# A fused attention and MLP block on one core: activation tables fetched ahead, first transposes in two banks, a Silu gate for the last tokens, and a new order

## The chip, the core and the metric

The kernel runs on one core of a Trainium2 chip. The core has a matrix engine (PE, with PEld for its weight loads), a vector engine (DVE), an engine for activation functions (ACT), GpSimd (POOL), and SyncE (SP), which here only issues transfers. The metric is the time of one launch in device microseconds; less is better.

## The reference

Input x is 2048 tokens of 448 values. With xn = layernorm(x), two branches are computed and joined:

```
A: q, k, v = xn @ wqkv             16 heads of 28
   token s attends to s, s-2, s-4, ... s-14 (those >= 0), softmax
   s = attention output @ wo
B: h = gelu_tanh(xn @ w1 + b1)     1792 hidden values
   g = silu(h @ w2 + b2)
out = x + s * g                    bf16 in and out
```

## The kernel before

Tokens are taken even ones first, then odd ones, so that a token attends to itself and its seven neighbours to the left. They form 16 tiles of 128 and four chunks of four tiles.

**The work.** For each tile: load, statistics on DVE (`bn_stats`), 1/sqrt(var) on ACT (chunk 0) or POOL (later chunks), xn on DVE, and xn transposed: by PE for the four tiles of chunk 0, by a transposing transfer of SP's queue for the others. Then the projections q, k and v (lines 532 and 556). q and k are copied out of PSUM to `qk_tok` and transposed by SP's queue to `qkT`; v is copied to `v_tok` and moved by POOL's transfers to where attention wants it.

ff1 makes h for a chunk of 512 tokens in 14 hidden tiles (line 591), gelu on ACT (595). ff2 (line 627) makes 448 outputs for one tile of tokens out of 14 hidden tiles; then `y` = that plus b2 on DVE (649), `t` = tanh(y/2) on ACT (655), `g` = (t+1)*y on DVE (659), which is twice silu(y). The last tile is cut into two halves of 224 columns.

Attention works on nine blocks of 228 tokens (block 4: 224). A visit S of PE makes the scores of a block in four banks (677); ACT takes exp (687) into `E`, POOL or DVE multiplies by the mask (693). A visit P makes the outputs in two banks, one for each window of 114 tokens (709). For each window DVE does four steps: transpose, reciprocal, transpose, multiply into `oT` (719, 723, 728, 733). A final (796) multiplies `oT` of a tile by wo; DVE makes `sg` = 0.5 * that * g (801) and `o` = x + sg (807), SP writes it out (811).

**PE's tile shapes.** The first batch of projections, transposes, ff2, finals and warm-ups use the whole array (128 rows). The other projections and ff1 run two at a time on its halves (64 rows): a `pair` has four steps, then a no-op on POOL or SP that passes a semaphore on (the hop), then three steps. Scores use 32 rows and 64 columns, attention outputs 64 rows and 32 columns.

**PSUM.** There are eight banks. A matmul task takes banks, and the evacuation gives them back.

**The order.** The kernel records tasks with costs, priorities (`PRIO`, `LATER`) and dependencies; a planner (`_Plan.run`) gives every task an engine and a place with a model of the times, and the instructions are written out in that order. On an engine nothing overtakes. So a change of a cost in the model moves instructions, though the cost itself issues none. The stages are: ff1 of chunks 0 and 1, attention of chunks 0 to 2, ff1 of chunk 2, attention of chunk 3, ff1 of chunk 3; ff2 and finals fill in.

**ACT's tables.** sqrt, gelu and exp each need a function table; tanh is in those of exp and gelu. A load is written right before the first activation that needs another table. `state["gate"]` and `exps` make the first exp of a stage wait for all gelus before it, and ff1 for all exps before it.

**Warm-up.** At the start PE runs matmuls on zeros, up to a planned time of 8 us (line 327).

Of the kernel before, what the change touches and what calls it, by code (L numbers as in the profile page):

```python
# [13 lines left out]
HOP = 0.10  # L14
# [6 lines left out]
MASK_ON = (("DVE", "POOL"), (0.4, 1.2))  # L21
# [23 lines left out]
class _Plan:  # L45
# [29 lines left out]
    def _at(self, t, e, free):  # L75
        at = free.get(e, 0.0)
        for p, n in t.take.items():
            if len(p.free) < n or p.fifo and p.fifo[0] is not t:
                return None
            at = max(at, sorted(p.free)[n - 1][0] + HOP)  # L80
        if t.table and self.table not in t.table:
            at += TABLE
        for d in t.deps:
            at = max(at, d.end - d.tail if d.on == e else d.end + HOP)
        if e == "PE" and t.mode != self.mode:
            at = max(at, free.get(e, 0.0) + SWITCH)
        return at

    def run(self):
# [9 lines left out]
        while ready:  # L99
            cand = []  # L100
            for t in ready:
                ways = []
                for e, c in zip(t.eng, t.cost):
                    at = self._at(t, e, free)
                    if at is not None:
                        ways.append((at + (c if len(t.eng) > 1 else 0.0), at, e, c))
                if ways:
                    _, at, e, c = min(ways)
                    cand.append((at, t, e, c))
            if not cand:  # L110
                raise RuntimeError("the plan is stuck: " + str([(t.seq, t.eng, t.fn.__qualname__) for t in ready[:20]]))
            first = min(cand, key=lambda k: k[0])
            near = [k for k in cand if k[2] == first[2] and k[0] <= first[0] + SLACK]
            tiled = first[2] == "PE" and self.mode < 64
            at, t, e, c = min(near, key=lambda k: (-k[1].prio - (TILED if tiled and k[1].mode < 64 else SAME if k[2] == "PE" and k[1].mode == self.mode else 0),
                                                   k[0], k[1].seq))
            if t.limit is not None and at > t.limit:
                t.fn, c = None, 0.0
            t.on, t.start = e, at
            if e == "PE" and t.fn is not None:  # L120
                self.mode = t.out or t.mode
            if t.table and self.table not in t.table:
                self.table = t.table[0]
            free[e] = at + c
            t.end = at + c + t.tail
            for p, n in t.take.items():
                got = sorted(p.free)[:n]
                for g in got:
                    p.free.remove(g)
                t.slots[p] = [g[1] for g in got]  # L130
                if p.fifo is not None:
                    p.fifo.pop(0)
            for p, owner, i in t.give:
                p.free.append((t.end, owner.slots[p][i]))
            ready.remove(t)
            order.append(t)
            for u in t.users:
                u.ndep -= 1
                if not u.ndep:
                    ready.append(u)  # L140
# [24 lines left out]
def kernel(  # L165
# [13 lines left out]
    P = 128  # L179
# [66 lines left out]
    def ring(name, n, shape, dt=BF16, fifo=False):  # L246
# [24 lines left out]
        "project": (49.5, 205, 104, 52.5,),  # L271
        "project2": (147, 150, 101, 61,),
        "values": (89.5, 62.5, 21, 58,),
        "attn": (185, 179.5, 78, 174.5, 106.5, 106, 138.5, 136.5, 32.5,),
        "ff1": (185, 180, 84.5, 176.5, 66.5, 64.5, 156.5, 189.5, 203, 146, 76, 114.5, 77.5, 179.5,
            75.5, 118.5, 180.5, 14.5, 163, 68, 151, 115.5, 194.5, 167.5, 180, 188.5, 86, 93,),
        "gelu": (62.5, 22.5, 95, 92.5,),
        "ff2": (144, 162.5, 103.5, 142.5, 44.5, 112.5, 67, 5, 89, 106.5, 101.5, 75, 74, 55, 11.5,
            6.5,),
        "final": (140, 19.5, 70.5, 47, 112, 34.5, 23.5, 142.5, 73, 53, 198.5, 188.5, 81.5, 126.5,  # L280
            180, 71,),
        "norm": (37.5, 132, 179.5, 129.5, 74.5, 99, 161, 69, 63, 62, 43.5, 73, -5.5, 90, 133.5,
            150,),
        "loads": (166.5, 166, 188, 139.5, 54.5,),
        "stats": (47.5, -60, 180.5, 23, 127, 56, 188.5, 77, 197.5, -13.5, 185, 205.5, 138, 14, 52.5,
            138.5,),
        "turn_x": (108.5, -1, 28, 116, 210, 116.5, 131.5, 160, 41.5, 79.5, 70, 119, -4.5, 74.5,
            132.5, 111,),
        "turn_qk": (68.5, 112, 174.5, 90, 80, 6, 149.5, 60.5, 4, 140.5, 199.5, 96.5, 103, 166.5,
            140, 156,),  # L290
        "move_v": (81.5, 95, 23, 95, 18.5, 26.5, 8, 128, 29.5,),
        "copies": (50, 119.5, 58.5, 76, 32.5, 135.5, 43, 1, 87, 79.5, 129, 77, 32, 41.5, 135,),
    }
    LATER = {"swap": 135, "qk": 165, "v": 29.5, "gelu": 30.5, "exp": 55.5, "mask": -60, "pv": 45, "recip": -16.5, "os": 54.5, "y": 153.5, "tanh": 182.5, "g": 58, "sg": 183, "o": 120.5}
# [28 lines left out]
    t_on = plan.add("DMA", 0.8, lambda _: None, (), 100)  # L323
# [6 lines left out]
    t_eps = plan.add("DVE", 0.07, memset("vector", eps_t[:], EPS), [t_on], prio=99)  # L330
    t_eps = plan.add("DVE", 0.07, memset("vector", half_t[:], -0.5), [t_eps], prio=99)
# [7 lines left out]
    t_qz = [plan.add("DVE", 0.08, memset("vector", q[:, :, :, DH:], 0.0), [t_on], prio=95) for q in qk_tok]  # L339
    t_vw = [plan.add("DVE", 0.08, memset("vector", v[:, :, DH:], 1.0), [t_on], prio=96) for v in v_tok[:9]]  # L340
    t_row0 = plan.add("POOL", 0.1, memset("gpsimd", row0[:], 0.0), [t_on], prio=93)
    t_row0 = plan.add("POOL", 0.1, memset("gpsimd", row0[:1, :], 1.0), [t_row0], prio=93)
    t_wo = [plan.add("POOL", 1.0, memset("gpsimd", wo[:], 0.0), [t_on], prio=93)]

    def dma(eng, dst, src, kb, prio, deps=(), issue=0.5, rate=350.0):
        def fn(_):
            {"SP": nc.sync, "ACT": nc.scalar, "POOL": nc.gpsimd}[eng].dma_start(dst, src)
        a = plan.add(eng, issue, fn, [t_on] + list(deps), prio)
        return plan.add("DMA", kb / rate, lambda _: None, [a], prio, tail=1.7)
# [16 lines left out]
    def load_x(t0, n, prio, eng="SP", deps=()):  # L366
        d = dma(eng, x_sb[:, t0:t0 + n, :],
                rows(x_half, t0 * P, n * P).rearrange("(t p) d -> p t d", p=P), 112 * n, prio, deps,
                rate=270.0 if t0 < TPC else 350.0)
# [7 lines left out]
    load_x(0, 1, 300, "SP")  # L377
    load_x(1, 1, 300, "ACT")
    t_w = []

    def load_w(kt, prio):
        t_w.append([dma("SP", w_in[:, kt, :], A_wqkv[kt * P:(kt + 1) * P, :], 336, prio, rate=270.0)])
# [6 lines left out]
    t_w.append([dma("SP", w_in3[:64], tails[:, 0:3:2, :], 112, PRIO["loads"][3], rate=270.0),  # L389
                dma("SP", w_in3[64:], tails[:, 1:3, :], 112, PRIO["loads"][3], rate=270.0)])  # L390
# [7 lines left out]


# [11 lines left out]
    t_rs = {}  # L411

    def rstds(t0, n):
        if t0 < TPC:
# [6 lines left out]
            b = plan.add("DVE", 0.16, f2, [a], prio=290)  # L421
        else:
# [13 lines left out]
    def norm(t, prio):  # L436
# [11 lines left out]
        halves = []  # L448
        for i in range(2):
            def f3(k, i=i):  # L450
                xn, tp = buf(p_xn, a), half_bank(buf(p_b, (halves or [k])[0]))
                for kt in (2 * i, 2 * i + 1):
                    nc.tensor.transpose(tp[:, kt, :], xn[:, kt * P:(kt + 1) * P], ident[:])
            halves.append(plan.add("PE", 0.13 if t else 0.22, f3, [twice if i else a, t_ident] + halves, prio, take=() if i else (p_b,),
                                   give=((p_xn, a, 0),) if i else (), tail=0.15))
        b = halves[0]

        n = 2 if t < 2 else 4
        for k0 in range(0, KT, n):
            def f4(k, k0=k0):  # L460
                copy(k.on, xnT[:, k0:k0 + n, t * P:(t + 1) * P], half_bank(buf(p_b, b))[:, k0:k0 + n, :])
            t_xT[t] = plan.add(("DVE", "ACT"), (dve(n * P, 2), act(n * P)), f4, [halves[(k0 + n - 1) // 2]] + ([t_xT01[t]] if k0 else []), prio,
                               give=((p_b, b, 0),) if k0 + n == KT else ())
            t_xT01.setdefault(t, t_xT[t])

# [135 lines left out]

    t_g = {}
# [13 lines left out]
    def ff2_part(t, cs, n, end, prio):  # L616
# [36 lines left out]

        def f3(k):
            nc.scalar.activation(buf(p_t, k)[:, :n], buf(pool, y)[:, :n], ACT.Tanh, scale=0.5)  # L655
        th = plan.add("ACT", act(n), f3, after, prio + LATER["tanh"], take=(p_t,), table=("exp", "gelu"))
# [86 lines left out]
    def attn(b, what):  # L743

        deps, take, give, fns, cost = [], [], (), [], -SWITCH
        for n, (w, blk) in enumerate(what):
            if not n or what[n - 1][0] != w:
                cost += SWITCH
            cost += 0.215
            if not n:  # L750
                cost += 0.03
# [40 lines left out]
    def final_part(t, cs, n, g, prio):  # L792
# [7 lines left out]
        def f2(k):  # L800
            nc.vector.scalar_tensor_tensor(out=buf(p_sg, k)[:, :n], in0=buf(p_b, a)[:, :n], scalar=0.5,  # L801
# [10 lines left out]
        q = plan.add("SP", 0.55, f4, [o], 50)  # L812
# [24 lines left out]
    for m, w1_, n, first in ((m_gen, m1[0], NW, None), (m_first, m1[1], NW, 0), (m_mid, m1[2], NW - 1, 1)):  # L837
# [10 lines left out]
        t_m = plan.add("POOL", 1.2 if first is None else 1.6, fn, [t_ident], prio=75)  # L848
# [34 lines left out]
    b1_at = plan.add("PE", 0.06, f_b1, [t_b1r, t_ident], 60, take=(p_b,), tail=0.15)  # L883
# [24 lines left out]
    for i, (c, what) in enumerate(STAGES):  # L908
        if what == "A":
# [3 lines left out]
            if i + 1 == len(STAGES) or STAGES[i + 1][1] != "A":  # L913
                state["gate"], state["early"] = gels, gels[:-1]
# [3 lines left out]
        else:  # L918
            if was == "A":
                gels = []  # L920
            hs = [ff1(c, mt, PRIO["gelu"][c], exps) for mt in range(NMT)]
# [3 lines left out]
            if c == 0:  # L925
                project(2)
                project(3)
            for t in range(c * TPC, (c + 1) * TPC):
# [38 lines left out]
```

## Time and profile before

| | us |
|---|---|
| three runs | 158.65, 158.05, 158.40; median 158.4 |
| span of the profiled execution, first to last instruction | 156.2 |
| the profiled execution's own time | not shown apart from the runs; median less span is 2.2 |
| PE busy (share of the span) | 150.1 (96%) |
| DVE busy | 113.2 (72%) |
| ACT busy | 83.3 (53%) |
| POOL busy | 74.7 (48%) |
| mean granted clock of PE | 1.000 |

A row of the timeline gives start, length, engine, line, operation, tiles, shape and count; in brackets stands idle time of the engine before it and what ended it. Neighbouring rows of PE overlap, since matmuls are pipelined; the time from start to start is what a row costs. The chain of waits goes back from the last instruction to whatever released each step.

### The profile page before, as it was taken

The numbers are of one execution on the slowest core, as the hardware profiler recorded it, in microseconds if no ns is written. First come the engines' busy times: TensorE is split into PE (matmuls) and PEld (weight loads), VectorE is DVE, ScalarE is ACT, GpSimd is POOL, SyncE is SP. The second block draws the span as 40 slices with busy tenths as digits, with TensorE's granted clock in tenths as the row PEclk, the third lists the DMA queues.
The fourth block names the chain that finished last, engine by engine and source line by source line (L and its number), as shares of the span: only waits on it lengthen the run. The fifth ranks groups of instructions, "written<-read, shape, count | busy, mean of one in ns | idle before, by whom it ended". The sixth has DMA issues, their size and how long they took to land.

```text
span 156.2 us, 5305 instructions
## 1 busy us (share of the span) xinstructions
PE 150.1 (96%) x2204; PEld 77.8 (50%) x2204; DVE 113.2 (72%) x259; ACT 83.3 (53%) x149; POOL 74.7 (48%) x123
## 2 busy tenths in 40 slices
PE   6999999999999999999999999999999999999980
PEld 2544454444455555455554644455556444545570
DVE  4789551486266758997799895109899996998992
ACT  3245867378889416444634149782496587051220
POOL 7854856000459408839261098389599780000000
PEclk9999999999999999999999999999999999999999
DMA  4999969999749443099039822123300100200211
GB/s 156 329 317 315 167 124 187 237 269 307 141 95 166 64 82 90 10 192 138 4 83 85 131 70 73 38 76 83 105 0 4 34 31 29 63 4 0 68 36 43
DMA packets 33575, 17.36 MB, mean 111 GB/s; under 512 B 25331, under 2 KB 32387, under 8 KB 33552
## 3 DMA queue, kind: packets, MB, share of 16 engines
q1 hardware_dynamic: 31472, 14.03, 41.3%
q0 software_dynamic: 1936, 2.88, 8.5%
q8 instruction: 17, 0.28, 0.8%
q10 hardware_dynamic: 144, 0.11, 0.2%
q14 instruction: 6, 0.05, 0.1%
HBM read 7.06 MB, written 1.84 MB: 57 GB/s over the span
## 4 chain that ended last, share of the span: by engine, by line
PE 80%; DVE 8%; DMA 3%; POOL 2%; issue 2%; ACT 1%; SPq 1%; DVEq 0%; ACTq 0%; POOLq 0%
PE bank L627 23%; PE bank L591 22%; PE bank L532 11%; PE bank L796 7%; PE bank L556 6%; PE bank L677 4%; PE bank L709 4%; PE bank L327 3%; DMA xnT<-xn 3%; POOL v L354 2%; DVE sg L801 2%; DVE o L807 1%; DVE w_in L659 1%; ACT E L687 1%; DVE xn L438 1%
## 5 line engine op out<-in xcount | busy, mean ns | idle before, releaser
L627 PE MATMUL bank<-w,h 128*128 128x448 bf16 (+1 forms) x238 | 45.2, 342 | 0.0
L591 PE MATMUL bank<-xnT,w 64*128 64x512 bf16 x392 | 44.7, 376 | 0.0
L595 ACT ACTIVATE h<-bank,b 128x512 bf16<-128x512 f32 x56 | 34.0, 689 | 12.9 <-PE bank L591 12.8
L354 POOL DMA_DIRECT2D v<-v_tok x52 | 27.6, 538 | 19.8 <-PE bank L709 9.0
L693 POOL TENSOR_TENSOR E<-E,m_gen 128x456 bf16<-128x456 bf16 x24 | 26.7, 1139 | 11.7 <-ACT E L687 9.5
L627 PEld LDWEIGHTS <-h 128*128 128x128 bf16 x238 | 22.3, 98 | 18.1 <-issue 0.4
L591 PEld LDWEIGHTS <-w 64*128 64x128 bf16 x392 | 19.1, 94 | 22.7 <-issue 1.1
L532 PE MATMUL bank<-w_in,xnT 64*128 64x448 bf16 (+1 forms) x212 | 24.3, 350 | 0.1
L687 ACT ACTIVATE E<-bank 128x456 bf16<-128x456 f32 (+1 forms) x36 | 17.0, 555 | 9.1 <-PE bank L677 9.1
L655 ACT ACTIVATE t<-y 128x448 f32<-128x448 f32 x15 | 8.7, 578 | 17.4 <-DVE y L649 17.4
L719 DVE STREAM_TRANSPOSE dt<-bank 128x480 f32<-128x480 f32 (+1 forms) x18 | 12.1, 671 | 5.6 <-PE bank L709 5.6
L532 PEld LDWEIGHTS <-xnT 64*128 64x128 bf16 (+1 forms) x212 | 10.6, 94 | 10.9 <-issue 1.1
L314 DVE CAST qk_tok<-bank 128x448 bf16<-128x448 f32 x16 | 9.4, 613 | 6.8 <-PE bank L532 6.8
L796 PE MATMUL bank<-wo,oT 128*128 128x448 bf16 (+1 forms) x68 | 14.1, 342 | 0.0
L312 ACT CAST qk_tok<-bank 128x448 bf16<-128x448 f32 x16 | 8.3, 533 | 10.6 <-PE bank L532 10.0
L556 PE MATMUL bank<-w_in,xnT 64*128 64x448 bf16 (+1 forms) x106 | 13.4, 349 | 0.0
L649 DVE TENSOR_TENSOR y<-bank,b 128x448 f32<-128x448 f32 x15 | 9.3, 620 | 4.9 <-PE bank L627 4.9
L728 DVE STREAM_TRANSPOSE dt<-rd 128x480 f32<-128x480 f32 (+1 forms) x18 | 12.1, 673 | 0.5
L733 DVE TENSOR_TENSOR oT<-bank,dt 128x456 bf16<-128x456 f32 (+1 forms) x18 | 11.3, 630 | 0.5
L404 DVE BATCH_NORM_STATS2 st<-x_sb 128x6 f32<-128x448 bf16 x16 | 9.6, 603 | 2.4 <-DMA x_sb<-in_A_x_dram 2.4
L438 DVE TENSOR_SCALAR xn<-x_sb,mv,rstd 128x448 bf16<-128x448 bf16 x16 | 6.3, 394 | 6.0 <-POOL rstd L426 5.8
L796 PEld LDWEIGHTS <-oT 128*128 128x128 bf16 x68 | 6.3, 98 | 6.3 <-issue 0.8
(62 smaller groups left out, 128.9 us busy)
## 6 DMA issues: line engine op xcount, KB each, us to landing
out_dram<-o SPq DMA_DIRECT2D x15, 112.0 KB, 1.7
w<-in_B_w_dram SPq DMA_DIRECT2D x2, 784.0 KB, 7.2
w<-in_B_w_dram SPq DMA_DIRECT2D x2, 672.0 KB, 7.0
x_sb<-in_A_x_dram SPq DMA_DIRECT2D x3, 448.0 KB, 6.3
v<-v_tok POOLq DMA_DIRECT2D x20, 64.0 KB, 2.5
w_in<-in_A_wqkv_dram SPq DMA_DIRECT2D x3, 336.0 KB, 4.3
w<-in_B_w_dram SPq DMA_DIRECT2D x4, 112.0 KB, 6.5
wo<-in_A_wo_dram POOLq DMA_DIRECT2D x4, 98.0 KB, 4.2
```

What stands on the lines that cost most here:

```text
L354: nc.gpsimd.dma_start(dst(k), src())
L532: return nc.tensor.matmul(ps[:, :D], xnT[r, kt, cs], w, start=start, stop=stop)
L556: return nc.tensor.matmul(ps[:, :D], xnT[r, kt, k0:k0 + P], w, start=start, stop=stop)
L591: return nc.tensor.matmul(ps[:], w1[r, kt, ms], xnT[r, kt, cs], start=start, stop=stop)
L595: nc.scalar.activation(buf(p_h, own, i)[:], buf(p_b, own, i)[:], ACT.Gelu_apprx_tanh, bias=b1[:, mt:mt + 1])
L627: nc.tensor.matmul(ps[:, :n], buf(*h_at[(c, mt)])[:, j * P:(j + 1) * P], w2[:, mt, cs], start=(mt == 0 and not biased), stop=(mt == NMT - 1))
L687: nc.scalar.activation(buf(p_E, k)[:, :n], buf(p_b, a, at + hl)[:, :n], ACT.Exp, scale=SCALE)
L693: (nc.gpsimd if k.on == "POOL" else nc.vector).tensor_tensor(out=E[:, :n], in0=E[:, :n], in1=m[:, :n], op=ALU.mult)
L719: nc.vector.transpose(buf(p_dt, k)[:, :32 * m], buf(p_b, po, i)[:, :32 * m])
L728: nc.vector.transpose(buf(p_dt, d)[:, :32 * m].rearrange("p (b c) -> p b c", c=32), buf(p_rd, r)[:, :m].unsqueeze(2).to_broadcast((P, m, 32)))
L733: nc.vector.tensor_tensor(out=oT[:, :, q0:q0 + 2 * nq], in0=buf(p_b, po, i)[:, :n].rearrange("p (l q) -> p l q", l=4), in1=buf(p_dt, d)[:, ...
L796: nc.tensor.matmul(ps[:, :n], oT[:, kt, t * P:(t + 1) * P], wo[:, kt, cs], start=(kt == 0), stop=(kt == KT - 1))
```

## The change

- One-column activations (`table`) are added: Gelu after the last sqrt (and after the last exp before a stage of ff1), Exp after the last gelu, Silu after the last gelu of chunk 3. Each brings its table load to its own place, and what needed the table now waits for it, ff1 on PE among them.
- For tiles 0 and 1 the two halves of the transposed xn go to two banks, so that their two copies don't depend on each other.
- For the four tiles of the last chunk, `t` and `g` become one Silu activation, and `sg` is a plain multiply.
- The planner's constants are changed (times from engine to engine, overlaps, costs of several tasks, rates of loads), and all priorities. All this acts through the order alone.

```diff
-HOP = 0.10
+HOP = 0.045
+RAW = 0.035
+OVERLAP = {"DVE": 0.084, "ACT": 0.115, "POOL": 0.04}
...
+        for d in t.deps:
+            at = max(at, d.end + HOP if d.on != e else d.end - d.tail if e == "PE" else d.end + RAW)
...
-            free[e] = at + c
+            free[e] = at + max(c - OVERLAP.get(e, 0.0), 0.0)
...
     PRIO = {
...
+    def table(name, func, deps):
+        return plan.add("ACT", 0.2, lambda _: nc.scalar.activation(sink[:], eps_t[:], func), [t_eps] + list(deps), prio=400,
+                        table=(name,))
...
-        halves = []
+        halves, apart = [], t < 2
         for i in range(2):
             def f3(k, i=i):
-                xn, tp = buf(p_xn, a), half_bank(buf(p_b, (halves or [k])[0]))
+                xn, tp = buf(p_xn, a), half_bank(buf(p_b, k if apart else (halves or [k])[0]))
...
+        if c == NCH - 1:
+            def f3(k):
+                nc.scalar.activation(buf(p_g, k)[:, :n], buf(pool, y)[:, :n], ACT.Silu)
+            t_g[t].append(plan.add("ACT", act(n) + 0.03, f3, after + [t_silu], prio + LATER["tanh"], take=(p_g,), give=held,
+                                   table=("silu",)))
+            return
...
+            if t >= NT - TPC:
+                nc.vector.tensor_tensor(out=buf(p_sg, k)[:, :n], in0=buf(p_b, a)[:, :n], in1=buf(p_g, g)[:, :n], op=ALU.mult)
+                return
...
-                state["gate"], state["early"] = gels, gels[:-1]
+                state["gate"], state["early"] = gels + [table("exp", ACT.Exp, gels)], gels[:-1]
...
-            if was == "A":
+            if was != "F":
                 gels = []
+                exps = exps + [table("gelu", ACT.Gelu_apprx_tanh, exps or t_sqrt)]
...
+            t_silu = table("silu", ACT.Silu, hs_done(c)) if c == NCH - 1 else None
```

The order on PE, before and after. T is the transpose of a tile, fb the first batch (q, k, v of tiles 0 and 1), q5 the projections q and k of tile 5, v45 those of v of tiles 4 and 5, f1.2.6 the pair of hidden tiles 6 and 7 of chunk 2, ff2.8 and fin.8 those of tile 8, S and P the visits of a block:

```
before: T0 fb T1 fb T2 fb q2.. T3 ..q2 b1 | f1.0.0 f1.0.2 q3 v23 f1.0.4 f1.0.6 f1.0.8 q6 q7 q5 q4
  f1.0.10 f1.0.12 f1.1.0 to f1.1.12 v45 v67 | S0 | ff2.1 | S1 | ff2.0 ff2.3.. ff2.5 ff2.2.. | P0 S2 |
  ..ff2.2 ..ff2.3 | q8 q9 q10 q11 | fin.0 | P1 S3 | ff2.6 ff2.4.. | P2 S4 | ..ff2.4 fin.2 | q14 q15 v1213
  v1415 q12 q13 | fin.3 fin.1 ff2.7.. | P3 S5 | ..ff2.7 fin.4 | v89 f1.2.0 to f1.2.12 v1011 | P4 P5 |
  ff2.9.. ff2.10.. fin.7 ..ff2.9 | S6 | ..ff2.10 ff2.8.. | S7 | ..ff2.8 ff2.11.. | P6 S8 | ..ff2.11 fin.8
  fin.5 | f1.3.0 f1.3.2 f1.3.4 | fin.6 | f1.3.6 f1.3.8 | fin.10 fin.11 | P7 P8 | f1.3.10 f1.3.12 |
  ff2.12 ff2.13 fin.12 fin.13 fin.9 ff2.14 fin.14 ff2.15 fin.15
after: T0 T1.. fb ..T1 fb T2 fb b1 T3 | fb q2 f1.0.0 q3 f1.0.2 v23 f1.0.4 to f1.0.12 v67 q6 q7 q5 f1.1.0
  f1.1.2 f1.1.4 v45 q4 f1.1.6 to f1.1.12 q9 q8 | S0 | ff2.2 | S1 | ff2.0 | P0 S2 | ff2.1 ff2.4.. | P1 S3 |
  ..ff2.4 ff2.6 ff2.3 | P2 S4 | ff2.5 fin.0 ff2.7 fin.1 fin.3 | q10 q11 v89 v1011 q12 q13 q14.. | P3 S5 |
  ..q14 | fin.4 fin.2 | q15 v1213 f1.2.0 to f1.2.12 | P4 P5 | ff2.10 ff2.11.. | S6 | ff2.9 fin.7 | S7 |
  ff2.8 | P6 S8 | ..ff2.11 fin.9 fin.8 fin.10 fin.6 fin.5 | f1.3.0 v1415 f1.3.2 to f1.3.12 | P7 P8 |
  ff2.14 ff2.13 fin.13 ff2.12 fin.14 fin.11 fin.12 ff2.15 fin.15
```

On SP's queue the loads of x for chunks 2 and 3 and both halves of w2 now stand together in front of the transposes of q and k of tiles 6, 7 and 5; before, the second half of w2 stood behind the first of these. ACT has the six one-column activations and one table load more, seven in all. The warm-ups are 12 instead of 17.

## Prediction

> **What bounds the kernel now.** I read the page first, then PE's timeline, the chain of waits, and the transfers of SP's queue. From the page:
>
> ```profile
> span 156.2 us, 5305 instructions
> ...
> PE 150.1 (96%) x2204; PEld 77.8 (50%) x2204; DVE 113.2 (72%) x259; ACT 83.3 (53%) x149; POOL 74.7 (48%) x123
> ...
> PE 80%; DVE 8%; DMA 3%; POOL 2%; issue 2%; ACT 1%; SPq 1%; DVEq 0%; ACTq 0%; POOLq 0%
> ```
>
> PE is the bound. Its timeline says how tightly (start, length, matmuls in the row):
>
> ```profile
> 45.55 0.70 PE L677 MATMUL bank<-qkT 32*64 32x57 bf16 x64
> 46.19 2.82 PE L627 MATMUL bank<-w,h 128*128 128x448 bf16 x14
> 48.94 0.70 PE L677 MATMUL bank<-qkT 32*64 32x57 bf16 x64
> 49.57 8.12 PE L627 MATMUL bank<-w,h 128*128 128x448 bf16 x42
> 57.62 0.68 PE L709 MATMUL bank<-E,v 64*32 64x57 bf16 x64
> ...
> 114.14 0.40 PE L677 MATMUL bank<-qkT 32*64 32x57 bf16 x6
> 114.76 0.65 PE L677 MATMUL bank<-qkT 32*64 32x57 bf16 x58 [0.22 <-ACT E L687]
> 115.34 2.82 PE L627 MATMUL bank<-w,h 128*128 128x448 bf16 x14
> ...
> 150.75 0.93 PE L796 MATMUL bank<-wo,oT 128*128 128x224 bf16 x8
> ```
>
> From start to start, 42 matmuls take 8.05 us and 14 take 2.75. The difference gives 0.189 each, so 14 are 2.65, and 0.10 goes at the change between tile shapes. Every change of shape in the trace costs this 0.10 to 0.11. A visit of scores takes 0.63; the one at 114.14 takes 1.20, so it lost 0.57. Summed so over all rows from 13.24 us on, PE loses only 1.3 us to waits: 0.57 here, 0.44 between 13.24 and 45.55 (a half of it at 27.3, for a transposed xn), 0.26 in three other visits of scores. So little else can be won in the middle. The end, from the chain:
>
> ```profile
> 151.58 0.40 DVE sg L801
> ...
> 152.28 0.31 DVE w_in L659
> ...
> 152.68 0.40 DVE sg L801
> ...
> 153.10 0.28 DVE o L807
> ```
>
> PE is done at 151.68 and DVE at 153.38, 1.70 later: DVE has a queue. The head, from the list of waits, and a transfer from SP's timeline:
>
> ```profile
> ACT xnT L312 <- DVE xnT L314: 0.8, 1, 0.8
> ```
>
> ```profile
> 27.02 0.51 SPq L347 DMA_DIRECT2D w<-in_B_w_dram  x1
> 27.63 5.22 SPq L360 DMA_TRANSPOSE qkT<-qk_tok  x1
> ```
>
> The second copy of the first transposed tile waits for the first. And a transpose issued behind three bulk loads (two of x, half of w2) held SP for 5.22 us.
>
> **How I cost it.** The matmuls stay the same but for five fewer warm-ups. I walked by hand along the changed order, engine by engine, with durations from these rows: 1.32 us for a pair of 448 columns, 1.51 of 512, 2.65 for an ff2 tile, 0.76 for a final, 2.26 of DVE for one window of attention output (133.80 to 136.06), 0.55 an exp, 0.60 a gelu, 1.14 a mask on POOL. "By the walk" means this. The new constants HOP, RAW and OVERLAP issue nothing; they act through the order.
>
> **Changes of shape.** The old order has 42, the new 32: the first transposes no longer cut into a pair, and finals no longer into ff1. 10 x 0.105 = 1.05 us less, on PE's path. Bounds 1.0 and 1.1.
>
> **The head.** Now all four transposes of tile 0 end at 6.22 before the first copy (6.26 to 6.55), and the first projection starts at 6.61. With two banks, xn is ready at 5.30 (an aggregate now stands ahead of it on DVE), two transposes end at 5.77, ACT's copy of 0.37 ends at 6.17: the projection starts at 6.21, 0.40 earlier. Not all is kept: the second slice of w_in lands at 7.94, and the walk uses it at 8.05. The load of the gelu table now stands on ACT in front of the evacuations of q0, q1 and v0: 9.87 to 11.35, one-column activation included, against 11.28 when the batch is done, so 0.1 late. At 13.38 PE has done what it had done at 13.24, and half a pair more (0.86): 0.72 ahead, of which 0.42 are four changes of shape counted above. 0.3 is the head's own; bounds 0 and 0.7.
>
> The row for that load is 15.41 to 16.69, with the first gelu at 16.71: 1.28 us and nothing after it. [...]
>
> **Tables ahead.** Six one-column activations (0.20 each, the row of L397) and a seventh load, for Silu: 2.5 us on an engine that is 53% busy. Of the six loads of before only the one at 111.5 reaches PE, in the 0.57 above. In the new order that load is over at 105.2 and its scores end at 107.6; what is late next is the tanh in front of the exps (108.25), then POOL's four masks, over at 113.4, where P6 wants them at 114.5: 1.1 to spare. The new wait is PE's: ff1 waits for the one-column activation, with all of PE behind it, with 0.5 (chunk 0), 1.4 (chunk 2) and 0.7 us (chunk 3) to spare. These gains and losses go into the stalls below.
>
> **The last gate.** Three STTs of 0.62 and two of 0.38 leave DVE: 2.6 us. Silu is not in the trace; tanh of the same shape is 0.58, gelu of 512 columns with a bias 0.69, and ACT has that room (5.16 busy of 19.20 in the last stage). Its table is there at 3.5 us after P7 starts, the first y at 5.4. But P7 and P8 now come after all of ff1, so DVE has less time: from P7's end, 4 windows x 2.26 = 9.0, three y 1.7, four sg and o 4.0, the last two halves 1.4, together 16.1, done 16.95 after P7's start, PE 15.96. DVE ends 1.0 after PE, not 1.7: 0.7 less. Bounds: 0 (DVE enters late) and 0.95 (only the last sg and o, 0.75, are left).
>
> **The new order's own stalls.** The walk finds six of 0.1 to 0.15 us, mostly where DVE frees a bank just as PE wants it: f1.2 pair 6 (P3's second window), S6 (P4's second window), ff2.8 (y), final 10, f1.3 pairs 2 and 4 (sg of finals 8 and 5). That is 0.7; where it resolves nothing under 0.1, I take the 1.3 that the old order loses, so no change; bounds 0.6 and 2.5. On SP the second half of w2 moved ahead of three transposes of q and k, and xn of tiles 9 and 8 stands behind those: the loads start 1.1 us earlier, the walk has tile 9 landed at about 42.7 and tile 8 at 44, and PE wants them at 44.35 and 45.1.
>
> **Sum.** 1.05 + 0.3 + 0.7 + 0 = 2.05 us: a span of 154.1. The runs lie at 158.05 to 158.65, median 158.4, 2.2 above the profiled span; the profiled execution's own time is not shown apart, so I take the difference as constant: 158.4 - 2.05 = 156.3.
>
> **Rivals.**
> (a) DVE is late. Between 104.6 and 132.5 it is busy 24.3 of 27.9 us, and the six places hang on it. If each costs 0.3 to 0.4 instead of 0.1, and the tail gives nothing: 1.5 + 0.7 more, 158.5; the middle of this case is 157.7. For it: the slacks above. Against: before, DVE was as busy in that stage, and of PE's waits there only one, the 0.57, was over 0.1. 0.20.
> (b) Slower: SP's queue. If transposes go only when all four loads have landed (35.58 of before, less 1.1, plus 784 KB at the 270 GB/s of those slices, 2.9: 37.4), and then one by one at the head's landing paces (qkT 16.31, 18.93, 21.41: 2.5; xnT 21.60 to 27.27: 1.9), tile 8 lands at 37.4 + 7.5 + 5.7 = 50.6, PE waits 5.5 us: 161.8. It decides from a landing at 45.1; from 48 the kernel is slower. For it: the 5.22. Against: before, three qkT issued beside w2's other half landed at 40.24, 40.99 and 41.80, 0.8 apart. 0.12.
> (c) PE's clock. Before, warm-ups of 512 columns come every 0.427 us and those of 128 every 0.107 up to 6.34; from 6.61 a 448 takes 0.19, so the pace doubles between. The new order has five warm-ups fewer, and PE idles some 0.6 us more before 6.2. If that idle made it begin the slow stretch (1.25 to 6.34, 5.1 us) anew, half of those 5.1 is lost: 2.55 more, 158.9. For it: fewer warm-ups stand in front of the same wait. Against: an idle of 0.3 us at 6.3 did not stop the doubling. 0.08. [...]
> [...] 0.05.
> The forecast has the remaining 0.55.
>
> **The numbers.** Best bounds together: 1.1 + 0.7 + 0.95 + 0.7 = 3.45, 154.9. Worst: 1.0 + 0 + 0 - 1.2, 158.6, which takes in (a) and (d); (b) and (c), 0.20 together, are left out. The runs of before scatter by 0.6 us, so 0.5%, 0.8 us, is about what can be told: faster is under 157.6, slower over 159.2. Faster: 0.55, a little over half of (a), half of (d): 0.69. Slower: most of (b), a little of (c): 0.12. The rest, 0.19, is the same.
>
> **What would show it.** In the changed kernel's profile: first projection near 6.2 and 448s at 0.19 from there; 32 changes of shape; no idle row of PE before tiles 9 and 8 of q and k; a score visit of 0.63 at about 107; DVE done some 1.0 after PE. A PE idle row over 1 us, a half pace after 6.6, or a first evacuation of q after 12 would prove me wrong.

## The result: slower by 0.4%, not faster by 1.3%

| | us | ratio to the kernel before, 95% |
|---|---|---|
| before, beside it | 158.23 (157.75 to 158.65) | |
| changed kernel | 158.98 (158.46 to 159.15) | 1.0044 (1.0022 to 1.0065) |
| forecast | 156.3 (154.9 to 158.6) | 0.987 |
| profiled execution of the changed kernel | 159.09, span 157.3 | |

One of the six executions of the changed kernel (166.42) is left out here, and every ratio below leaves out executions more than 1.5% above the fastest of the same kernel.

The 0.4% is within the 0.5% that the forecast took for what can be told from three runs; with six executions of one kernel and five of the other, the interval lies above 1.

The page of the changed kernel (its lines have new numbers: ff1 602, q and k 543, v 567, ff2 641, scores 698, attention outputs 730, finals 815, mask 714, `y` 663, `g` 680, `oT` 754, `sg` 823 and, for the last chunk, 821, `o` 829, SP's transposes 361, the hop 501):

```profile
span 157.3 us, 5299 instructions
...
PE 149.0 (95%) x2199; PEld 89.0 (57%) x2199; DVE 111.4 (71%) x255; ACT 84.8 (54%) x156; POOL 71.8 (46%) x122
...
PE 60%; DVE 19%; DMA 11%; SPq 4%; issue 3%; ACT 1%; DVEq 0%
```

PE held 80% of the chain and holds 60%; DVE, transfers and SP's queue took the rest. PE's timeline shows where (start, length, matmuls in the row, idle before it and who ended that):

```profile
45.07 0.93 PE L543 MATMUL bank<-w_in,xnT 64*128 64x448 bf16 x8 [0.46 <-DMA xnT<-xn]
46.22 2.07 PE L543 MATMUL bank<-w_in,xnT 64*128 64x448 bf16 x20 [0.22 <-DMA xnT<-xn]
...
68.89 0.60 PE L698 MATMUL bank<-qkT 32*64 32x56 bf16 x52
69.93 0.25 PE L698 MATMUL bank<-qkT 32*64 32x56 bf16 x12 [0.45 <-issue]
...
85.74 2.07 PE L543 MATMUL bank<-w_in,xnT 64*128 64x448 bf16 x20 [0.96 <-SPq L501]
...
110.32 0.70 PE L698 MATMUL bank<-qkT 32*64 32x57 bf16 x64
...
118.98 0.65 PE L698 MATMUL bank<-qkT 32*64 32x57 bf16 x58 [0.30 <-DVE oT L754]
...
128.46 1.78 PE L602 MATMUL bank<-xnT,w 64*128 64x512 bf16 x14 [0.46 <-DVE sg L823]
```

From end to end of neighbouring matmuls, less the time of one, the losses are: 0.63 and 0.39 for xn of tiles 9 and 8; 0.60 inside the scores of block 4, where the profile shows nothing that PE waits for; 1.13 for a hop that SP was to pass on; 0.47 in the scores of block 8; 0.62 and 0.08 before ff1's second and third pair of chunk 3, and 0.2 more there; smaller ones 0.5. That is 4.6 us. The forecast had 1.3.

The end did what was forecast. The last steps of the chain:

```profile
153.47 0.40 DVE sg L821
...
153.89 0.03 DVE o L829
...
154.08 0.39 DVE sg L821
...
154.50 0.28 DVE o L829
```

PE is done at 153.74, DVE at 154.78: 1.04 later, where it was 1.70.

The balance of the two traces: 1.05 less in changes of shape (42 to 32, counted), 0.2 less in the head (at 13.49 PE is 0.61 ahead of the old order, of which 0.42 are four of those changes), 0.66 less between PE's end and DVE's, 0.3 less between DVE's end and the last instruction, 3.3 more in stalls: 1.1 more, and the spans are 156.2 and 157.3.

### The profile page after: what moved, and what is told of

It reads as the page before. It is cut to its first block, busy times and chain, and to the rows that moved or that the text cites. A ratio compares the mean times of both kernels' runs of the same rounds, so it can differ in the third digit from the quotient of the medians.

```text
span 157.3 us, 5299 instructions
## 1 busy us (share of the span) xinstructions
PE 149.0 (95%) x2199; PEld 89.0 (57%) x2199; DVE 111.4 (71%) x255; ACT 84.8 (54%) x156; POOL 71.8 (46%) x122
## 4 chain that ended last, share of the span: by engine, by line
PE 60%; DVE 19%; DMA 11%; SPq 4%; issue 3%; ACT 1%; DVEq 0%
PE bank L641 21%; PE bank L602 16%; PE bank L543 9%; PE bank L815 5%; DMA x_sb<-in_A_x_dram 4%; PE bank L567 4%; DMA w_in<-in_A_wqkv_dram 4%; SPq L361 3%; DMA xnT<-xn 3%; PE bank L730 3%; DVE st L411 3%; PE bank L698 3%; DVE dt L749 2%; DVE dt L740 2%; DVE g L680 2%
## 5 line engine op out<-in xcount | busy, mean ns | idle before, releaser
L602 PE MATMUL bank<-xnT,w 64*128 64x512 bf16 x392 | 45.7, 376 | 0.5 <-DVE sg L823 0.5
L641 PE MATMUL bank<-w,h 128*128 128x448 bf16 (+1 forms) x238 | 44.7, 342 | 0.0
L602 PEld LDWEIGHTS <-w 64*128 64x128 bf16 x392 | 26.6, 94 | 16.2 <-issue 1.5
L543 PE MATMUL bank<-w_in,xnT 64*128 64x448 bf16 (+1 forms) x212 | 25.6, 350 | 2.0 <-SPq L501 1.0
L714 POOL TENSOR_TENSOR E<-E,m_gen 128x456 bf16<-128x456 bf16 x21 | 22.2, 1087 | 6.7 <-ACT E L708 6.1
L543 PEld LDWEIGHTS <-xnT 64*128 64x128 bf16 (+1 forms) x212 | 13.1, 94 | 10.2 <-DMA xnT<-xn 1.6
L676 ACT ACTIVATE t<-y 128x448 f32<-128x448 f32 x12 | 6.9, 579 | 21.8 <-DVE y L663 21.8
L567 PE MATMUL bank<-w_in,xnT 64*128 64x448 bf16 (+1 forms) x106 | 14.0, 349 | 0.0
L815 PE MATMUL bank<-wo,oT 128*128 128x448 bf16 (+1 forms) x68 | 13.4, 341 | 0.0
L446 DVE TENSOR_SCALAR xn<-x_sb,mv,rstd 128x448 bf16<-128x448 bf16 x16 | 7.3, 454 | 5.1 <-DMA xnT<-xn 4.6
L315 DVE CAST v_tok<-bank 128x448 bf16<-128x448 f32 x7 | 4.3, 620 | 8.0 <-PE bank L567 8.0
```

The lines of the kernel that those rows point to most:

```text
L543: return nc.tensor.matmul(ps[:, :D], xnT[r, kt, cs], w, start=start, stop=stop)
L567: return nc.tensor.matmul(ps[:, :D], xnT[r, kt, k0:k0 + P], w, start=start, stop=stop)
L602: return nc.tensor.matmul(ps[:], w1[r, kt, ms], xnT[r, kt, cs], start=start, stop=stop)
L641: nc.tensor.matmul(ps[:, :n], buf(*h_at[(c, mt)])[:, j * P:(j + 1) * P], w2[:, mt, cs], start=(mt == 0 and not biased), stop=(mt == NMT - 1))
L714: (nc.gpsimd if k.on == "POOL" else nc.vector).tensor_tensor(out=E[:, :n], in0=E[:, :n], in1=m[:, :n], op=ALU.mult)
L815: nc.tensor.matmul(ps[:, :n], oT[:, kt, t * P:(t + 1) * P], wo[:, kt, cs], start=(kt == 0), stop=(kt == KT - 1))
```

## The experiments

The theory after this reading: the change's own parts give what the forecast says, and the order loses it again in four ways (DVE beside masks, tiles 9 and 8, hops on SP, the stop in block 4), each of which can be taken away by a small edit. The rival: the order has no slack anywhere, so that a stall taken away comes back at the next place. The kernels of 14 to 16 are the kernel before with one part of the change; all others are the changed kernel. Where steps of its order were moved, it was done after planning, like this (shortened; the landing of a moved transfer moves along):

```diff
     plan.run()
+    base = list(plan.order)
+    for i, j in moves:          # step i is written out right ahead of step j
+        plan.order.remove(base[i])
+        plan.order.insert(plan.order.index(base[j]), base[i])
```

**1 and 2. More instructions ahead of PE's stop.**

```diff
+    first = (the first transposes of tile 0)
+    first.fn: for _ in range(8):     # 20 in the second kernel
+        nc.tensor.matmul(bank[:, :1], warm[:, :P], warm[:, :1], start=True, stop=True)
```

The stop is the 0.60 us inside the visit that makes block 4's scores: 1.23 us from 68.89 on where others take 0.63. That PE waits there for its own instructions, and stops at other places when more of them stand ahead, was the author's guess, which no trace had shown; the rival is a wait for a bank.

> The changed kernel with eight more one-column warm-up matmuls ahead of the first transposes (TensorE is idle there from 4.74 to 5.30 us), and nothing else; every later TensorE instruction stands 16 places further on in its stream. [...] Rival: the stop is a wait for the bank of ff2.3, which VectorE frees at 69.86, 0.07 before TensorE goes on. Then the visit stays at 1.2 and the time at 159.0.

> The same with twenty one-column matmuls, 40 instructions further. [...] Rival (a bank or a data wait at 69.3): 1.2 us for the scores of block 4 as now, no new stretch, 159.0 to 159.3.

With forty more, five of ten executions took 163.8 to 165.3. The other five give 1.0001 (0.9964 to 1.0039), an interval that overlaps the changed kernel's. In the profiled one (158.00) the scores of block 4 ran through, and VectorE's `y` of ff2.3, the rival's releaser, ended only at 69.16, behind them:

```profile
68.19 0.70 PE L698 MATMUL bank<-qkT 32*64 32x56 bf16 x64
```

```profile
68.54 0.62 DVE L663 TENSOR_TENSOR y<-bank,b 128x448 f32<-128x448 f32 x1
```

The rival falls. But no new stop came behind block 3's scores either, where the guess had asked for one.

With sixteen more, five of six executions took 163.9 to 165.1 (one 157.54), and the profiled one, of the five, shows something else, on DVE and POOL:

```profile
61.38 6.89 DVE L680 SCALAR_TENSOR_TENSOR g<-t,y 128x448 bf16<-128x448 f32 x1
```

```profile
61.72 6.06 POOL L714 TENSOR_TENSOR E<-E,m_gen 128x456 bf16<-128x456 bf16 x6
```

A `g` that takes 0.62 us elsewhere was not done until 0.49 us after the sixth of six masks. In the changed kernel's own trace the same `g` began at 61.21 and the masks at 62.39. So the order has put it where a delay of about a microsecond decides between nothing and six. PE paid for it twice: block 4's scores took 5.81 us, waiting for banks, and from 72 to 78 us the granted clock was 0.50, so that 14 matmuls of ff2 took 4.77 us where they take 2.82. On the stop this kernel says nothing.

**3. The second half of w2 behind six transposes.** `moves = [(load of w2's second half, the step behind xn of tile 8)]`

> The changed kernel with one step moved on SP: the load of the second half of w2 is issued behind the transposes of q and k of tiles 6, 7 and 5 and of xn of tiles 10, 9 and 8, in place of ahead of them. Theory: the 0.63 and 0.39 us that q and k of tiles 9 and 8 wait (matmuls at 45.07 and 46.22; xn landed at 45.03 and 46.17) come from the first of those transposes being held 5.62 us behind four bulk loads, the last of which landed at 37.51. With three loads ahead it should be held some 3.5 to 4.5 us, tiles 9 and 8 should land 1 to 3 us earlier (42 to 44.5), the two waits should be gone and the kernel take 158.0 to 158.2. Rival: the transposes are bound by their own pace (1.2 to 3.8 us from one landing to the next, beside the moves of v on POOL at 39.7 to 41.5), whatever is ahead: then tile 9 lands after 44.5 still and no more than 0.4 is won, 158.7 or above.

The time moved the other way. The waits for tiles 9 and 8 were gone (the tiles landed at 44.37 or before), and the load, which now landed at 47.34, held the transposes behind it: DVE waited 2.58 us for a buffer of xn, the masks of block 0 came late, and PE lost 0.85 at 54.91; then came a `g` of 5.94 us, begun inside the first of six masks, and the executions took 161 to 168. A move on SP that was right for two tiles was paid for by those behind them.

**4. The hops of tiles 12 and 13 ahead of a transpose.** `moves = [(transpose of q, k of tile 11, the step behind both hops)]`

> The changed kernel with one step moved on SP: the transpose of q and k of tile 11 (issued 83.39 to 85.63) stands behind the two hops that the second halves of q and k of tiles 12 and 13 wait for, in place of ahead of them. Theory: the 1.13 us that TensorE waits at 85.74 is this hop, over at 85.69, which is ready some 84.0 but stands behind the transpose in SP's order. The wait should be gone, and the kernel take 157.9 (1.1 less) to 158.3 where a part is lost again later. Rival: something else is late there too (the banks of q and k of tile 12, VectorE behind its g of 1.49 us at 79.97), and half of the wait or more stays: 158.5 to 159.0.

1.0101 (1.0048 to 1.0154), from three executions (three more took 164.6 to 166.6): not faster. The wait at 85.74 was gone, and one of the same size stood at another hop, on SP behind the last four of these five transposes (the two moved hops stand behind the first):

```profile
94.42 0.74 PE L567 MATMUL bank<-w_in,xnT 64*128 64x448 bf16 x6 [1.02 <-SPq L501]
```

```profile
82.70 10.98 SPq L361 DMA_TRANSPOSE qkT<-qk_tok  x5
```

Here the rival of no slack was right: given back nine microseconds later.

**5. No masks on POOL.**

```diff
+    for t in plan.order:
+        if t.on == "POOL" and (t is a multiply by the mask):
+            t.fn = None
```

> The changed kernel without the multiplies by the mask that GpSimd does (21 of them, 1.09 us each; those that VectorE does stay). The output of these heads is then not masked. Theory: VectorE's operations whose operands all lie in SBUF (xn, g, o) do not run while GpSimd multiplies; in the changed kernel's trace they take 1.29 (xn at 67.31), 0.99 (o at 115.30), 1.47 (g at 116.21), 0.67 and 1.06 us (o at 122.89 and 124.66) beside masks, and 0.39, 0.62 alone, while operations that read a bank keep their 0.62 to 0.68 beside masks. Without the masks all of these should be at 0.39 and 0.62, the scores of block 8 (1.10 us at 118.46, waiting for a bank that VectorE frees) be back at 0.63 to 0.75, the wait of 0.62 us at 128.46 be 0.2 or less, and the kernel take 157.6 to 158.2; the g at 79.97 stays at 1.4 to 1.5, since it stands beside GpSimd's o, not a mask. Rival: VectorE has too much to do there in any case (it is busy 99% from 110 to 128 us): the two waits stay at 0.4 or more each, and the time at 158.6 to 159.2.

0.9960 (0.9935 to 0.9985), 157.19, and all twelve executions within 156.5 to 158.5. Two operations of DVE took 0.99 and 1.47 in the changed kernel:

```profile
115.30 0.99 DVE L829 TENSOR_TENSOR o<-x_sb,sg 128x448 bf16<-128x448 bf16 x1
116.21 1.47 DVE L680 SCALAR_TENSOR_TENSOR g<-t,y 128x448 bf16<-128x448 f32 x1
```

Here they take 0.39 and 0.62, and the scores of block 8 run through:

```profile
114.45 0.39 DVE L829 TENSOR_TENSOR o<-x_sb,sg 128x448 bf16<-128x448 bf16 x1
114.76 0.62 DVE L680 SCALAR_TENSOR_TENSOR g<-t,y 128x448 bf16<-128x448 f32 x1
```

```profile
117.61 0.70 PE L698 MATMUL bank<-qkT 32*64 32x57 bf16 x64
```

The wait at 128.46 is gone, the `g` beside POOL's `o` still takes 1.49, as expected, and block 4's scores still lose 0.60. Not all of the 1.8 us gained is DVE's, though: the hop that lost 1.13 lost 0.2 here, for which no cause is shown.

**6. The hops on ACT.** `-(nc.gpsimd if k.on == "POOL" else nc.sync).nop()` becomes `nc.scalar` for those of SP.

> The changed kernel with every hop that stood on SP (the empty instruction between the two halves of a pair) on ScalarE at the same place in the order. Theory: hops on SP are late because they queue behind transposes of 1.2 to 2.6 us; moving one transpose only shifted the wait from 85.74 to 94.42. On ScalarE nothing of the kind is ahead: the waits of 1.13 us at 85.74 and 0.16 at 96.86 go, none comes at 94.4, and the kernel takes 157.7 to 158.0. Rival: the hop is late because of what is behind it in the chain (ScalarE's exps and evacuations, 0.5 to 0.7 each, are then ahead of it): TensorE waits 0.3 us or more at several hops and the time is 158.5 or above.

1.0124 (1.0076 to 1.0171) from two executions; of the two others, 164.82 and 167.67, the first was profiled, with a `g` of 6.80 us beside six masks. In its rows no matmul waits for a hop any more. The time had to wait for a kernel in which that `g` is out of the way.

**7. Tile 10 later, that `g` earlier.** `moves = [(xn of tile 10, xn of tile 11), (g of ff2.1, oT of block 0's second window), two moves of v into the run of masks]`

> The changed kernel with two steps moved: on SP the transpose of xn of tile 10 goes behind those of tiles 9, 8, 15 and 13 (its first use is at 77 us), and VectorE's g of ff2.1 goes ahead of the second window of block 0, so before GpSimd's run of six masks, of which two moves of v are now in the midst. Theory: tiles 9 and 8 land 1.2 us earlier, at 43.2 to 45.0, and of the 1.02 us at 45.07 and 46.22 no more than 0.3 is left; the g, which took 6.89 us beside the six masks in the trace with sixteen more instructions and 0.61 in the changed kernel's own, takes 0.6 to 1.6. Time 158.0 to 158.4. Rival: landing is bound by the 16 transfer engines (busy 90% up to 41 us), not by the place in SP's order: the tiles land as before, and the time is 158.8 to 159.2.

1.0097 (1.0060 to 1.0135), from five of six executions (the sixth 161.44). PE no longer waits for tiles 9 and 8. But the earlier place of the `g` lies beside earlier masks: it took 3.44 us (59.28 to 62.72; three masks, 58.80 to 61.85), and PE waited 1.50 for the bank of the `oT` behind it. Block 4's scores did not stop, after a stretch of ff2 that had become 1.5 us longer.

**8. All repairs, with the `g` as in 7.** Further moves on DVE: `[(two steps of block 5's second window, o of final 7), (o of final 8, o of final 5), (g of ff2.11, o of final 5)]`

> The changed kernel with all repairs: twenty one-column matmuls more (block 4's scores were 0.63 with them), the two moves, the hops on ScalarE, and on VectorE two local changes of order: the second window of block 5 ahead of o and g at 115.3 to 117.7, and the sg of finals 8 and 5 ahead of an o and a g. Theory: the forecast failed by these four kinds of stall alone, so that without them the forecast's own gains show: 0.60 + 1.0 + 1.3 + 0.47 + 0.6, 4.0 us less than 159.0: 155.0, or up to 156.3 where a third of it is lost again at a next place. Rival: the new order has no slack, and what is taken away at one place is lost at the next (as the moved transpose did): 157 or above.

1.0004 (0.9984 to 1.0025). The waits of the list were gone from the trace or down to 0.1, and one `g` of 3.46 us beside three masks took most of it back: PE lost 1.78 at 64.30, for the bank behind it. Experiment 9 puts that to the test.

**9. All repairs, and the masks behind the `g`.** The `g` is back at its place, and the first of the six masks waits for it:

```diff
+    mask_next.fn: behind(mask, g)      # a semaphore from DVE to POOL
```

> All repairs as in the run before, but VectorE's g of ff2.1 stands at its old place (behind the second window of block 0) and the moves of v too; in their stead the first of GpSimd's six masks waits for this g, so that the run of masks can't begin ahead of it. Theory: with all repairs the kernel stayed at 158.1 because the g, placed earlier, took 3.46 us beside three masks and the stretch of ff2 matmuls before block 4's scores took 8.44 us (61.25 to 69.69) where 6.66 do in the changed kernel. With the mask held behind it the g takes 0.62, the stretch 6.7 to 7.0, and the kernel 156.2 to 156.7. Rival: what bounds that stretch is VectorE's work as such; it stays at 8 us or the loss turns up in the scores of block 4, and the time is 157.5 or above.

0.9875 (0.9833 to 0.9918), 156.45 us, six executions between 155.73 and 156.71, beside 158.15 for the kernel before. The whole interval lies below the kernel before and below the changed kernel's. Its page:

```profile
span 154.5 us, 5340 instructions
...
PE 81%; DVE 12%; DMA 4%; issue 1%; SPq 1%; DVEq 0%
```

**10 to 13. One repair taken back at a time.** The first asks whether block 4's scores, 0.63 us with the twenty matmuls, stop for 0.60 again without them.

> The kernel with all repairs (156.45), less one: without the twenty one-column matmuls, so that every TensorE instruction stands 40 places earlier, as in the changed kernel. [...] Rival (bank or data wait): 0.63 as with them, because all banks and transposes are the same; time 156.4 or below (twenty matmuls less).

> The kernel with all repairs, less one: VectorE's order at 114 to 128 us as in the changed kernel (o and g ahead of block 5's second window; sg of finals 8 and 5 behind an o and a g). Theory: the scores of block 8 take 1.10 again and the wait before ff1's second pair of the last chunk is 0.6 again, with o and g at 0.99 and 1.47 beside masks: 0.47 + 0.55 less what the repair itself cost at final 9 (0.25): 157.1 to 157.5. Rival: the order doesn't matter, VectorE's sum does: 156.3 to 156.7.

> The kernel with all repairs, less one: hops on SP again. Theory: the wait of 1.1 to 1.25 at 84 to 86 us is back (SP's hop behind two transposes), and 0.1 to 0.2 at 95 to 97: 157.5 to 157.8. Rival: with tile 10's transpose elsewhere SP is not late there, and less than 0.4 comes back: 156.4 to 156.8.

> The kernel with all repairs, less one: the transpose of xn of tile 10 ahead of those of 9 and 8 again. Theory: the waits for tiles 9 and 8 are back, 0 to 1.2 us in sum (they were 1.02, 1.17 and 1.5 in three traces and none in two with the same order), so 156.5 to 157.6, with more scatter between executions. Rival: no wait comes back, 156.4.

| taken back | PE's loss there: changed, all repairs, taken back | ratio to before | executions left out of the ratio |
|---|---|---|---|
| nothing (9) | | 0.9875 (0.9833 to 0.9918) | 0 of 6 |
| twenty matmuls | 0.60, 0, 0.60 | 0.9928 (0.9905 to 0.9950) | 7 of 12, 158.9 to 160.0 |
| DVE's order | 0.47 + 0.70, 0 + 0.10, 0.47 + 0.71 | 0.9950 (0.9928 to 0.9973) | 2 of 12, 159.3 and 160.2 |
| hops on ACT | 1.13, 0, 1.29 | 0.9980 (0.9954 to 1.0006) | 0 of 12 |
| tile 10 later | 1.02, 0, 0 | 0.9925 (0.9893 to 0.9956) | 2 of 11, 158.4 and 159.9 |

The first three losses come back at their place and size. The row that tells most is block 4's, without the twenty matmuls, at the same 52nd matmul:

```profile
68.41 0.60 PE L698 MATMUL bank<-qkT 32*64 32x56 bf16 x52
69.46 0.25 PE L698 MATMUL bank<-qkT 32*64 32x56 bf16 x12 [0.45 <-issue]
```

The last is undecided in its trace (no wait in the profiled execution, 155.62 us), while its executions scatter from there to 159.9; in the changed order tiles 9 and 8 land within a microsecond of when PE wants them.

Two limits. The table's times rest on the ratios, not on single profiles: the profiled executions without the twenty matmuls and with DVE's old order have a span of 154.6, against 154.5 for 9, since what came back there was met by less elsewhere (block 0's scores began 0.25 and 0.53 earlier, and DVE's new order itself costs PE 0.24 at a final). And without the twenty matmuls most executions, seven of twelve, took some 3 us more than the other five, as long as the changed kernel; none of them was profiled, so what they lose is not shown, and the 0.60 explains the other five alone.

The executions of 163.8 and more follow the `g` that met six masks. They came in the changed kernel (1 of 6) and in experiments 1, 2, 3, 4 and 6 (5 of 6, 5 of 10, 5 of 6, 3 of 6, 2 of 4), where the `g` stands as in the changed kernel; the three that were profiled (1, 3, 6) all show it at 5.94 to 6.89. In 5, without masks, in 7 and 8, with the `g` elsewhere, and in 9 to 13, with the masks behind it, none of 83 executions is above 161.5. So the changed order costs more than its median says: now and then it takes 5 to 7 us longer. That the unprofiled ones have this cause is inferred from this pattern.

**14 to 16. The parts alone, in the old order.**

> The kernel before, its order kept, with the Silu gate alone: for tiles 12 to 15 one Silu on ScalarE at the place of the tanh, no STT on VectorE, and the Silu table fetched by a one-column activation behind the last gelu. By the forecast's term: VectorE is done 1.70 us after TensorE before, and loses 2.6 us of work in front of the end, so it ends 0.4 to 1.0 after TensorE and the time falls by 0.7 to 1.3, to 156.7 to 157.3. Rival: the end is set by the last tile's chain (last matmul, Silu, sg, o, store) and not by VectorE's queue, or the load of the Silu table delays the first gate: a fall of 0.3 or less, 157.6 to 158.

```diff
+    for each gate g of tiles 12 to 15: tanh dropped, g = nc.scalar.activation(Silu) at its place
+    last gelu: nc.scalar.activation(sink[:], eps_t[:], ACT.Silu) behind it
```

0.9950 (0.9924 to 0.9975), 0.8 us less. PE is done at 152.03 and DVE at 153.07, against 151.68 and 153.38 before:

```profile
152.38 0.39 DVE sg L801
...
152.79 0.28 DVE o L807
```

DVE ends 1.04 behind PE again, as in the changed kernel, and the gain is about the forecast's 0.7.

> The kernel before, its order kept, with the second transposes of tiles 0 and 1 in a bank of their own alone. By the forecast's term: the first copy no longer waits for the second transposes, and the first projection starts at 6.2 to 6.3 instead of 6.61; but the second slice of w_in lands near 8, so that 0 to 0.3 of it is kept: 157.6 to 158.0. Rival: the first projection starts as before, because xn, not the bank, sets it: 157.9 to 158.1.

```diff
-half_bank(buf(p_b, (halves or [k])[0]))
+half_bank(p_b.bufs[5 + t] if i and t < 2 else buf(p_b, (halves or [k])[0]))
```

0.9982 (0.9955 to 1.0010). The first projection starts at 6.40 instead of 6.61; what remains after the second slice of w_in can't be told from nothing.

> The kernel before, its order kept, with one-column activations alone, each at the end of a group of exps or gelus and with the next group's table (five of them). By the forecast only the load at 111.5 reaches TensorE, in the 0.57 us that the scores at 114.14 lose: that visit falls from 1.20 to 0.65 us or so, and the time to 157.4 to 157.8. Rival: the loads only move ahead of other work on ScalarE (tanh, evacuations) and delay that: no change or up to 0.4 slower, 157.9 to 158.4.

```diff
+    behind the last exp or gelu of each group: nc.scalar.activation(sink[:], eps_t[:], next table's function)
```

0.9999 (0.9967 to 1.0032). The scores at 114 fell from 1.20 to 0.63 as forecast. ACT and PE show what that was paid with:

```profile
45.15 1.28 ACT L941 ACT_TABLE_LOAD   x1
46.44 0.20 ACT L941 ACTIVATE sink<-eps_t 128x1 f32<-128x1 f32 x1
46.55 0.95 ACT L312 CAST v_tok<-bank 128x448 bf16<-128x448 f32 x2
```

```profile
47.12 1.11 PE L627 MATMUL bank<-w,h 128*128 128x448 bf16 x5 [0.77 <-ACT v_tok L312]
```

The load went ahead of an evacuation whose bank ff2 needs: 0.57 won, 0.8 lost.

## Why the prediction was wrong, point by point

**Changes of shape, the last gate: right.** There are 32 changes, though no experiment takes them alone; DVE ends 1.04 behind PE; the Silu gate alone gave 0.8.

**Tables ahead: right in the trace, and worth nothing alone.** The scores at 110.32 took 0.63, without the old order's 0.57, and no ff1 waited for a one-column activation. As the only change (16) it gave 0.9999: what the scores won was lost at an evacuation behind the moved load.

**The head: right in kind.** First projection at 6.08 (forecast 6.21), first evacuation of q at 11.42 (11.35); 0.2 of the 0.3 was kept. Rival (d), a drain of ACT at each table switch, is shown by no run: before, the first gelu begins at 16.71, right behind the load that ends at 16.69, and here the load took 10.02 to 11.30 and the one-column activation began at 11.31. Its chance of 0.05, and the half of it in the 0.69 for faster, stand on no trace. Rival (c) did not happen in the head: from 6.08 on a matmul of 448 columns took 0.19 us there, none twice that. Half pace did come later, in the profiled execution of experiment 1, with a granted clock of 0.50 from 72 to 78 us (0.979 in the mean of that execution), behind the long `g`.

**"The new order's own stalls": this is the step that failed.** It was put at no change, with 2.5 us in all as the worst; it was 4.6. Without this term the forecast stands: 2.2 us gained in the trace, and 0.9875 measured once the four are repaired, against the forecast 0.987. So close a match is in part luck: of the 2.2 the forecast had no term for 0.3, the stretch behind DVE's end, the repairs have costs of their own, and the interval is 0.4% wide on either side.

It failed in three ways. First, the walk gave DVE's `g`, `o` and `xn` the durations they have alone. This line of the kernel before's groups was there to be read (busy, then the mean in ns):

```profile
L659 DVE SCALAR_TENSOR_TENSOR w_in<-t,y 128x448 bf16<-128x448 f32 x7 | 6.7, 960 | 0.4 <-ACT t L655 0.3
```

960 ns for what takes 620 alone: four of those seven stood beside masks, at 1.07 to 1.46. In the old order no row of PE names them as what it waited for; in the new one PE waits for banks that come free behind them: 0.47 and 0.70. Experiments 5 and 11 show it. In the changed kernel's trace `sg`, `y` and `oT`, which read a bank, kept 0.58 to 0.63 beside masks, while `o` and `g`, with two inputs in SBUF, went up to 1.06 and 1.47, and an `xn` to 1.29. These durations beside masks should have been weighed as part of rival (a).

Second, the walk looked for SP's cost at tiles 9 and 8 only, had them landed at 42.7 and 44 (they landed at 45.03 and 46.17), and rival (b) priced one big wait. There were several small ones: 1.02 there, 1.13 and 0.16 at hops, because a hop on SP waited its turn behind transposes that held SP 1.2 to 2.5 us each (1.19 at 69.25 and 2.24 at 83.39 in the changed kernel, 2.53 at 94.93 in experiment 4). The recorded working has no term for a hop as an instruction with a queue ahead of it.

Third, rivals (a) and (b) were priced as alternatives to the forecast. They came together, each at a fraction of its worst case, so the range, whose upper end took in only one of them, ended 0.4 below the measured median.

The stop of 0.60 inside the scores of block 4 was in no step. It depended on how many of PE's instructions stand ahead: it came at the same matmul, with the same 0.60, in the changed kernel and in 4, 5 and 10, and in none of the six with forty more (2, 8, 9, 11 to 13). That it also depends on how fast those ahead ran is suggested by 7 alone, which has the old count, a longer stretch of ff2 and no stop. That PE waited there for its own instructions is the author's guess, which no run shows. The changed kernel's page has a queue of instruction transfers, `q8 instruction: 17, 0.28, 0.8%` (transfers, MB, share); in its trace one of them moved between 67.4 and 67.8 us and none from 67.8 to 70, while PE stood still from 69.49 to 69.93.

## What to carry to other kernels

Cost an operation at the duration it has beside the neighbours it will have, not alone: read the group's mean against its shortest (960 ns against 620 here), and ask which other engine is busy in the long ones. An order that packs the bound engine more tightly can also remove the slack that hid small delays elsewhere (PE's waits went from 1.3 to 4.6 us here). Where two steps must not meet, a dependency that holds the meeting off (a mask that waits for a `g`) can be surer than another place: here moving the `g` only brought it to other masks (3.44 and 3.46 us). A passing no-op belongs on the queue whose instructions ahead of it are shortest (here 1.13 and 1.29 us lost on SP, nothing at that place on ACT). And look at all executions of a kernel, not at the median alone.

## What was not expected of the hardware

- A `g` of DVE, with two operands in SBUF and 0.62 us long alone, was held off by a whole run of POOL's multiplies, not by one: 1.47 where one mask had begun (changed kernel, 116.21), 3.44 from inside the first of three (experiment 7), 5.94 from inside the first of six (3), 6.89 where six began just behind it (1). POOL's transfers of v beside it cost it nothing (changed kernel, 0.61 at 61.21).
- A transpose on SP held the queue 1.2 us at the least (1.19 at 69.25 in the changed kernel), 2.2 in the mean of five in experiment 4 (10.98 together), and 5.62 for one behind four bulk loads (changed kernel, 29.50).
- PE stood for 0.60 us inside block 4's scores where the profile shows nothing that it waits for, and with forty more instructions ahead of it they ran through in 0.63 (experiment 9; without them, in 10, the 0.60 is back).
- After the 5.81 us in which PE did little but wait (experiment 1), the granted clock was 0.50 from 72 to 78 us: in that execution 14 matmuls of ff2 took 4.77 us where they take 2.82, about two more microseconds.
